# Three moved steps in a fused attention and feed-forward kernel: row loads, copies of x, a late split

## The chip, the core and the metric

The kernel runs on one core of a Trainium2 chip. A core has a matrix engine (TensorE, PE in the profile; its weight loads are PEld), a vector engine (VectorE, DVE), a scalar engine (ScalarE, ACT), GpSimd (POOL) and SyncE (SP), which here only issues DMAs. The engines run their own instruction lists and wait for one another by semaphores. The metric is the time of one execution in device microseconds.

## The reference, cut to what matters

```python
xn = _layernorm(x, axis=-1)            # x: 1 x 2048 x 512, f32
s = _A_ref(xn, A_wqkv, A_wo)           # softmax attention, 32 heads of 16
g = _silu(_B_ref(xn, ...))             # (silu(xn @ w_gate) * (xn @ w_up)) @ w_down
return x + s * g
```

## The kernel before, in words

All products are made on TensorE from values split in two parts (a high part rounded for the engine and the low remainder), three matmuls for each product. The 2048 tokens are four blocks of 512 (`NB`), each of four tiles of 128 (`NT`).

**The first stage** (L779 to L880) normalises x, transposes it and makes q, k and v, block by block. A block has twelve slots, `n` = 0 to 11, each one tile of work on TensorE with twelve 128x512 matmuls: eight feature tiles (`feature_tile`, L738, four of q and four of k) and four value tiles (`value_tile`, L753). In block 0 the value tiles come first; in the others they come last, n = 8 to 11. Around each slot the loop hands small steps to the other engines:

- `load_tile` (L541) reads 128 rows of x into `xin` (the tile `facc` in the profile), which has room for one block. `load_x` (L544) does it for four tiles. SyncE issues these loads in program order between the stores of q and k (`q_d`, `k_d`, L749).
- `stats` and `rates` (L610, L615) are mean and variance of the rows on VectorE, with a square root on ScalarE.
- Block 1 is normalised by `norm` (L628, VectorE, into `xn`, two buffers), one tile at a time, transposed on TensorE (`turn_x`, L655, by L638) and split (L649 ScalarE, L652 VectorE). Blocks 2 and 3 are normalised in place by `norms` (L663, ScalarE), transposed in sixteen pieces on VectorE (`turn_quarter`, L671, into `xw`) and split by `split_block` (L676), four casts on ScalarE (L679) and four subtractions on VectorE (L680).
- `copy_fx` (L771, ScalarE, L777) copies block 0's transposed x in sixteen pieces into `fx`, the layout of the feed-forward part. The source of the copies is the buffer that block 2 is split into.
- `feature_tile` has ScalarE square the sums and cast them (L745, L746), VectorE subtract (L747) and SyncE store both parts. The products stand in `ps`, which has four buffers; `parts` has four buffers too.
- While weights last, `split_w` (L565) has ScalarE cast a weight tile (L574) and GpSimd subtract (L575).

**The second stage** is attention, cut in 101 steps (`run`, numbered by `now`), with the feed-forward products and, from step 89 on, the output projection laid between the score matmuls (L187). The output projection of block b (`project_out`) takes steps 89 to 92 for b = 0, 93 to 96 for b = 1 and 97 to 100 for b = 2, twelve pairs of matmuls in each step. Its left operands, written (b, c), are the attention output split in two parts by `split_out` (L323), a cast and a subtraction on VectorE, queued in `chores` and run between the copies `pr<-acc` of scores (L999, L1005), or at the step's end (`tidy`, L138). The dictionary in `out_splits` (L352) says at which step each split is queued; here `early` is 87, `opened[units - 2]` is 92 and `opened[units - 1]` is 96. GpSimd gates each finished output tile (L361, L362).

Of the kernel before, what the change touches and what calls it, by code (L numbers as in the profile page):

```python
# [27 lines left out]
NT = TB // P  # L28
# [15 lines left out]
EPS = 1e-5  # L44
FINE = (30,)
TURNS = (0, 0, 0, 0, 0, 2, 4, 6, 8, 10, 13, 16, 16)
QSLOT = (0, 1, 0)
KSLOT = (0, 0, 1)

# [2 lines left out]
def tile_block(ctx: ExitStack, tc: tile.TileContext, x, wqkv, wo, w_gate, w_up, w_down, out):  # L52
# [42 lines left out]
    def load_rows(dst, src, slots):  # L95
        for h in range(2):
            for s, part in enumerate(slots):
                r = h * HALF + 2 + s * DH
                sp.dma_start(dst[r:r + DH].bitcast(F32),
                             src[part].rearrange("(j h d) t -> h d j t", j=2, h=2)[h])  # L100
# [5 lines left out]
    def load_q(u, i=None):  # L106
        g, b = divmod(u, NB)
        load_rows(qst[u % 2 if i is None else i], q_d[:, g * 64:(g + 1) * 64, b * TB:(b + 1) * TB], QSLOT)

# [37 lines left out]
    def load_wd(i):  # L147
        raw = one.tile([P, D], F32, tag="wdr", name="wdr")
        sp.dma_start(raw, w_down[(i % NF) * P:(i % NF + 1) * P])
        wdr[i] = raw  # L150
# [172 lines left out]
    def split_out(b, c):  # L323
        dst, src = lhs[b, c], parts_o[b, c]

        def rest():
            dve.tensor_sub(dst[1], src, dst[0].bitcast(F32))  # L327
            ready.add((b, c))

        chores.append((2, partial(dve.tensor_copy, dst[0], src)))  # L330
        chores.append((3, rest))
# [19 lines left out]

    def out_splits():  # L352
        for b, c in {early + 1: ((0, 0), (0, 1)), early + 2: ((0, 2),), early + 3: ((1, 0),), early + 4: ((1, 1),),
                     early + 5: ((1, 2),), opened[units - 2] + 1: ((2, 0),), opened[units - 2] + 2: ((2, 1),),
                     opened[units - 2] + 3: ((2, 2),)}.get(now, ()):
            split_out(b, c)
        if now - opened[units - 1] - 2 in range(EARLY):
            gate_rest(now - opened[units - 1] - 2)
# [37 lines left out]
    def gate_rest(t):  # L396
        chores.append((3, partial(dve.scalar_tensor_tensor, facc[:, t], facc[:, t], 0.5, gate[t], op0=ALU.mult, op1=ALU.mult)))
        chores.append((3, partial(dve.tensor_add, facc[:, t], facc[:, t], last[t])))
# [59 lines left out]
    units = NG * NB  # L458
# [7 lines left out]
    now = -1  # L466
# [17 lines left out]
    early = len(sizes) - EARLY - (NB * NT - NT)  # L484

    blocks, opened = [], []
# [40 lines left out]
    with ExitStack() as pro:  # L527
# [13 lines left out]
        def load_tile(t):  # L541
            sp.dma_start(xin[:, t % NT], x[t * P:(t + 1) * P])

        def load_x(b):  # L544
            for t in range(NT):
                load_tile(b * NT + t)
# [81 lines left out]
        def norm(t, parts=1):  # L628
            xn[t] = two.tile([P, D], F32, tag="ga", name="xn")
            n = D // parts  # L630
            for i in range(parts):
                w = slice(i * n, (i + 1) * n)
                made = dve.tensor_scalar(xn[t][:, w], xin[:, t, w], mv[:, t, 0:1], rs[:, t:t + 1], op0=ALU.subtract, op1=ALU.mult)
            return made
# [137 lines left out]
        def copy_fx(i):  # L772
            i, w = divmod(i, 2)
            i, u = divmod(i, 2)
            j, h = divmod(i, 2)
            dst = fx[halves[h], j].rearrange("p (c u) t -> u p c t", u=2)[u]
            nc.scalar.copy(dst[:, 2 * w:2 * w + 2], xt[0][j][halves[u], 2 * w:2 * w + 2])  # L777

        pend = []  # L779

        def add():
# [8 lines left out]
        for b in range(NB):  # L790
            more = b + 1 < NB
            slots = [(feature_tile, m) for m in range(8)]
            slots = [(value_tile, t) for t in range(NT)] + slots if b == 0 else slots + [(value_tile, t) for t in range(NT)]
            for n, (make, i) in enumerate(slots):
                if b == 0:
                    if n + 5 < 12:
                        load_w(worder[n + 5])
                    if n >= 2 and n + 2 < 12:
                        split_w(worder[n + 2], pool)
                if b == 0 and n == 2:  # L800
                    load_x(1)
                if more and b:
                    for part in range(TURNS[n], TURNS[n + 1]):
                        turn_quarter(part)
                if b == 2 and n in (6, 7):
                    load_gu(n - 6)
                if b == 2 and n == 8:
                    load_wd(0)
                if not more and n == 2:
                    split_gu(0)  # L810
                    tidy()
                    for bank in acc:
                        dve.memset(bank, 0.0)
                if not more and n in (1, 3):
                    load_k(0, n // 2)
                if not more and n == 5:
                    load_q(0)
                if not more and n == 6:
                    for c in range(2):
                        load_v(0, c)  # L820
                made = make(b, i)
                if b == 0 and n == 2:
                    split_x(0, 0, xf)
                if b < 2 and 0 <= 12 * b + n - 3 < 16:
                    copy_fx(12 * b + n - 3)
                if n == 0 and b:
                    flush(b - 1)
                if make is feature_tile:
                    pend.append(made)
                if b == 0 and n == 11:  # L830
                    ring(0, 2, one)
                    queries(0, one)
                if more and b:
                    if n < 2:
                        stats(2 * n)
                        stats(2 * n + 1)
                    if n == 1:
                        rates(0, NT)
                    if n in (2, 3):
                        norms(2 * n - 4)  # L840
                    if n == 10:
                        split_block(b + 1)
                elif more:
                    if 2 <= n < 6:
                        stats(n - 2)
                    if n == 5:
                        rates(0, NT)
                    if 6 <= n < 10:
                        norm(n - 6)
                    if 7 <= n < 11:  # L850
                        turn_x(b + 1, n - 7)
                if n == 10 and b < 2:
                    load_x(b + 2)
                if n == 8 and not more:
                    flush(b)
                if not more and n == 8:
                    dve.reduce_max(pk, peak, axis=AX.X)
                    dve.tensor_add(sm, pk[:, 0:1], pk[:, 1:2])
                if not more and n == 9:
                    tops = pps.tile([P, 512], F32, tag="ps", name="tops")  # L860
                    nc.tensor.transpose(tops[0:1, :P], sm, ident)
                    dve.reduce_max(s4, tops[0:1, :P], axis=AX.X)
                    dve.tensor_scalar(s4, s4, 0.51, None, op0=ALU.mult)
                    dve.tensor_scalar(flag, s4, LIMIT, None, op0=ALU.is_le)
                    dve.tensor_scalar(sel[:, :NG * NB], row[:, :NG * NB], s4, None, op0=ALU.mult)
                    for h in range(2):
                        dve.tensor_copy(selq[:, h * HALF:h * HALF + 1], s4)
                    fill(3 * DC)
                    tidy()
                    low, high = [pps.tile([P, 512], F32, tag="ps", name="low") for _ in range(2)]  # L870
                    mm(high[:2 * NG * NB, :8], sel, row[:, :8], start=True, stop=True, skip_group_check=True)
                    mm(low[:HALF + 2, :8], selq, row[:, :8], start=True, stop=True, skip_group_check=True)
                    act(shift, high[:2 * NG * NB, 0:1].to_broadcast([2 * NG * NB, 512]), AF.Copy, scale=-1.0)
                    for h in range(2):
                        two_rows = slice(h * HALF, h * HALF + 2)
                        act(qst[0][two_rows], low[two_rows, None, 0:1].to_broadcast([2, 2, 512]), AF.Copy, scale=-1.0)
                    for j in range(4):
                        pool.dma_start(sh_d[:, j * 512:(j + 1) * 512], shift.bitcast(F32))
                    fast = nc.values_load(flag, min_val=0, max_val=1)
# [53 lines left out]
    now = 0  # L933
# [93 lines left out]
    for now, (u, first, n) in enumerate(blocks):  # L1027
        g, b = divmod(u, NB)
# [101 lines left out]
```

## Time and profile before

| what | value |
|---|---|
| median of 3 runs | 1403.2 us (1402.9 to 1404.54) |
| the profiled execution, its own time | 1403.09 us |
| its span, first to last instruction | 1401.3 us |
| TensorE busy | 1392.0 us, 99% |
| ScalarE / VectorE / GpSimd busy | 1089.7 / 772.9 / 90.6 us |
| TensorE share of the chain that ended last | 87% |
| granted TensorE clock | 1.000 |

A row of the timeline reads: start in us, duration in us (of the whole group where there are several), engine, line of the kernel, operation, what is written and read, shapes, the count, and in brackets how long the engine had been idle before it and whose work ended the wait. A row of a table by windows gives the busy time of each engine in that stretch, the clock, the DMA share and GB/s. Matmuls overlap one another, so the step from one start to the next is the measure of TensorE's pace.

### The profile page before, as it was taken

Reading aid. Unit: us, or ns where it says so; the run is one execution under the profiler, and the core shown is the slowest. Engines: PE = TensorE matmul, PEld = TensorE weight load, DVE = VectorE, ACT = ScalarE, POOL = GpSimd, SP = SyncE. Lnnn points to the kernel's source line nnn. Section 1 sums busy time; section 2 is a strip of 40 time slices with the busy share of each in tenths; the row PEclk is TensorE's granted clock in tenths of the full one; section 3 lists DMA queues with packets and bytes.
Section 4 is the critical chain, followed back from the end, with each engine's and each line's share of the span. In section 5 each row is a group of like instructions: output and inputs, shape, how many; then the busy total and the mean of one; then the engine's idle time right before and its main releaser. Section 6 shows DMA issues by size and latency. Waiting matters only on the chain.

```text
span 1401.3 us, 27683 instructions
## 1 busy us (share of the span) xinstructions
PE 1392.0 (99%) x11193; PEld 841.9 (60%) x11193; DVE 772.9 (55%) x1301; ACT 1089.7 (78%) x1245; POOL 90.6 (6%) x104
## 2 busy tenths in 40 slices
PE   9999999999999999999999999999999999999998
PEld 7777756655655665565556556655565565565554
DVE  6575555355645653556456635554565446556655
ACT  6753578778888877787888778778877887788885
POOL 4200200000000000000000000000000000000333
PEclk9999999999999999999999999999999999999999
DMA  7678741043534511254514303356234113224423
GB/s 227 233 265 262 184 114 43 13 109 88 128 91 115 121 43 36 50 132 96 138 53 112 93 13 73 76 146 146 61 73 113 34 46 73 66 88 141 125 99 113
DMA packets 126954, 148.14 MB, mean 106 GB/s; under 512 B 12524, under 2 KB 79340, under 8 KB 126052
## 3 DMA queue, kind: packets, MB, share of 16 engines
q1 hardware_dynamic: 121620, 125.79, 35.0%
q0 software_dynamic: 4912, 20.12, 3.8%
q8 instruction: 89, 1.46, 0.4%
q14 instruction: 45, 0.37, 0.1%
q10 hardware_dynamic: 288, 0.39, 0.1%
HBM read 106.68 MB, written 39.58 MB: 104 GB/s over the span
## 4 chain that ended last, share of the span: by engine, by line
PE 87%; DVE 0%; ACT 0%; issue 0%; DVEq 0%
PE acc L405 32%; PE bankx L187 25%; PE score L940 17%; PE banky L187 10%; PE acc L940 3%; ACT pr L946 0%; PE acc L1067 0%; PE banky L1067 0%; PE score L1067 0%; DVE wd L143 0%; DVE wd L327 0%; DVE y L1074 0%; DVE y L368 0%; DVE pr L1005 0%; DVE pr L999 0%
## 5 line engine op out<-in xcount | busy, mean ns | idle before, releaser
L946 ACT ACTIVATE pr<-score 128x1024 f32<-128x1024 f32 x856 | 810.6, 1031 | 229.1 <-PE score L940 227.9
L405 PE MATMUL acc<-pr,vst 128*17 128x512 f32 x4096 | 461.9, 593 | 0.0
L940 PE MATMUL score<-qst,kst 50*128 50x512 f32 x1712 | 390.9, 413 | 0.1
L187 PE MATMUL bankx<-fx,guh 64*128 64x512 f32 x896 | 333.4, 393 | 0.1
L187 PE MATMUL banky<-fx,guh 64*128 64x512 f32 x896 | 324.7, 393 | 0.0
L405 PEld LDWEIGHTS acc<-pr,vst 128*17 128x17 f32 x4096 | 108.6, 97 | 286.3 <-issue 262.3
L940 PEld LDWEIGHTS score<-qst,kst 50*128 50x128 f32 x1712 | 175.2, 184 | 148.7 <-issue 68.9
L999 DVE COPY pr<-acc 128x512 f32<-128x512 f32 x168 | 116.2, 692 | 190.9 <-PE acc L940 187.1
L187 PE MATMUL bankx<-wd,hh 64*128 64x512 f32 x672 | 200.0, 392 | 0.0
L187 PE MATMUL banky<-wd,hh 64*128 64x512 f32 x672 | 197.7, 392 | 0.0
L187 PEld LDWEIGHTS bankx<-fx,guh 64*128 64x128 f32 x896 | 166.4, 186 | 19.3 <-issue 0.9
L187 PE MATMUL banky<-fx,gul 64*128 64x512 f32 x448 | 175.3, 391 | 0.0
L187 PE MATMUL bankx<-fx,gul 64*128 64x512 f32 x448 | 175.3, 391 | 0.0
L1013 ACT ACTIVATE pr<-pr 128x1024 f32<-128x1024 f32 x168 | 172.5, 1078 | 0.0
L187 PEld LDWEIGHTS banky<-fx,guh 64*128 64x128 f32 x896 | 166.3, 186 | 4.5
L1005 DVE COPY pr<-acc 128x512 f32<-128x512 f32 x168 | 116.1, 691 | 72.7 <-PE acc L940 57.2
L240 DVE SCALAR_TENSOR_TENSOR ga<-th,bankx 128x512 f32<-128x512 f32 x56 | 38.5, 688 | 178.5 <-ACT th L239 178.5
L940 PE MATMUL acc<-qst,kst 50*128 50x512 f32 x336 | 135.1, 402 | 0.3 <-DVE pr L999 0.3
L187 PEld LDWEIGHTS bankx<-wd,hh 64*128 64x128 f32 x672 | 124.9, 186 | 12.3
L187 PEld LDWEIGHTS banky<-wd,hh 64*128 64x128 f32 x672 | 124.4, 186 | 4.1
L187 PEld LDWEIGHTS bankx<-fx,gul 64*128 64x128 f32 x448 | 83.6, 187 | 11.8
L187 PEld LDWEIGHTS banky<-fx,gul 64*128 64x128 f32 x448 | 83.5, 186 | 2.3
(180 smaller groups left out, 1324.9 us busy)
## 6 DMA issues: line engine op xcount, KB each, us to landing
gur<-in_B_w_gate_dram SPq DMA_DIRECT2D x56, 256.0 KB
gur<-in_B_w_up_dram SPq DMA_DIRECT2D x56, 256.0 KB
wdr<-in_B_w_down_dram SPq DMA_DIRECT2D x56, 256.0 KB
kst<-k_d SPq DMA_DIRECT2D x192, 64.0 KB
qst<-q_d SPq DMA_DIRECT2D x192, 64.0 KB
fx<-xt_d SPq DMA_DIRECT2D x24, 512.0 KB
q_d<-parts SPq DMA_DIRECT2D x16, 512.0 KB
k_d<-parts SPq DMA_DIRECT2D x16, 512.0 KB
```

What stands on the lines that cost most here:

```text
L187: mm(banks[i], lhs[halves[i]], rhs[halves[i]], start=start, stop=stop)
L240: dve.scalar_tensor_tensor(ga, th, 1.0, bankx, op0=ALU.add, op1=ALU.mult)
L405: mm(acc[0][h * 32:h * 32 + DH + 1], v[:, kt % CT, h * (DH + 1):(h + 1) * (DH + 1)], probs[kt, h // 2][:, h % 2], start=kt == 0, stop=kt = ...
L940: mm(bank, k[r, j, kc * P:(kc + 1) * P], qst[u % 2][r, j], start=True, stop=True)
L946: act(pr, score[slot], AF.Exp, scale=0.25)
L999: dve.tensor_copy(probs[kt, j][:, 0], spare_bank)
L1005: dve.tensor_copy(probs[kt, j][:, 1], spare_bank)
L1013: act(probs[kt, j], probs[kt, j], AF.Exp, scale=0.25)
```

## The change

Four edits, all of order; no instruction is added or taken away.

1. Block 2's four row loads leave `load_x` at n = 10 of block 0 and are issued one by one at n = 7, 8, 9, 10, each behind the step that last reads its part of `xin`.
2. Block 1's `norm` of tiles 0 and 1 moves from n = 6 and 7 to n = 5 and 6; tiles 2 and 3 stay at 8 and 9.
3. The sixteen `copy_fx`, one a slot from n = 3 of block 0 to n = 6 of block 1, are spread by the table `COPIES`: six in block 0 (n = 3, 4, 5, 6, 10, 11), ten in block 1 (one each at n = 0, 1, 4, 5, 6, 7, two each at n = 8 and 9).
4. Four of the splits of the output projection move: (1, 2) from step 92 to 93, (2, 0) from 93 to 94, (2, 1) from 94 to 95, (2, 2) from 95 to 97.

```diff
+COPIES = ((0, 0, 0, 1, 1, 1, 1, 0, 0, 0, 1, 1), (1, 1, 0, 0, 1, 1, 1, 1, 2, 2, 0, 0))
...
         for b, c in {early + 1: ((0, 0), (0, 1)), early + 2: ((0, 2),), early + 3: ((1, 0),), early + 4: ((1, 1),),
-                     early + 5: ((1, 2),), opened[units - 2] + 1: ((2, 0),), opened[units - 2] + 2: ((2, 1),),
-                     opened[units - 2] + 3: ((2, 2),)}.get(now, ()):
+                     early + 6: ((1, 2),), early + 7: ((2, 0),), early + 8: ((2, 1),), early + 10: ((2, 2),)}.get(now, ()):
...
+        copied = list(range(16))
...
-                if b < 2 and 0 <= 12 * b + n - 3 < 16:
-                    copy_fx(12 * b + n - 3)
+                for _ in range(COPIES[b][n] if b < 2 else 0):
+                    copy_fx(copied.pop(0))
...
-                    if 6 <= n < 10:
-                        norm(n - 6)
+                    if n in (5, 6, 8, 9):
+                        norm((5, 6, 8, 9).index(n))
                     if 7 <= n < 11:
                         turn_x(b + 1, n - 7)
-                if n == 10 and b < 2:
+                        load_tile(2 * NT + n - 7)
+                if n == 10 and b == 1:
                     load_x(b + 2)
```

On VectorE, in block 0 from n = 5 to n = 8, stood before (`rs` is the last of `rates`, `xn` a normalised tile, `parts` the second half of a feature tile, `xt` the low part of block 1's transposed x):

```order
L626 SCALAR_TENSOR_TENSOR rs_168<-nw_169,rs_168 128x4
L747 TENSOR_TENSOR parts_400<-ps_387,parts_400 128x512
L633 TENSOR_SCALAR xn_407<-facc_83,mv_165,rs_168 128x512
L747 TENSOR_TENSOR parts_424<-ps_411,parts_424 128x512
L633 TENSOR_SCALAR xn_431<-facc_83,mv_165,rs_168 128x512
L652 TENSOR_TENSOR xt11_163<-acc0_80,xt10_162 128x4x128
```

And now, at the same place:

```order
L626 SCALAR_TENSOR_TENSOR rs_168<-nw_169,rs_168 128x4
L633 TENSOR_SCALAR xn_383<-facc_83,mv_165,rs_168 128x512
L747 TENSOR_TENSOR parts_402<-ps_389,parts_402 128x512
L633 TENSOR_SCALAR xn_409<-facc_83,mv_165,rs_168 128x512
L747 TENSOR_TENSOR parts_426<-ps_413,parts_426 128x512
L652 TENSOR_TENSOR xt11_163<-acc0_80,xt10_162 128x4x128
```

Each of the two normalisations stands one feature subtraction earlier. On SyncE, at the end of block 0, stood before the last q store, three k stores and then the four loads of rows (`facc`):

```order
L749 DMA q_d_59<-parts_424 128x2x512
L749 DMA k_d_60<-parts_454 128x2x512
L749 DMA k_d_60<-parts_484 128x2x512
L749 DMA k_d_60<-parts_512 128x2x512
L542 DMA facc_83<-in_A_x_dram 128x512 x4
```

And now:

```order
L749 DMA q_d_59<-parts_426 128x2x512
L542 DMA facc_83<-in_A_x_dram 128x512
L749 DMA k_d_60<-parts_454 128x2x512
L542 DMA facc_83<-in_A_x_dram 128x512
L749 DMA k_d_60<-parts_484 128x2x512
L542 DMA facc_83<-in_A_x_dram 128x512
L749 DMA k_d_60<-parts_512 128x2x512
```

The fourth load follows the last of these stores, where the first one stood. On VectorE, in steps 92 and 93 (`wd` holds the parts of block 1's operands and `hh` those of blocks 0 and 2; the first three rows belong to step 92 and the rows from the first L999 on to step 93), stood before:

```order
L451 TENSOR_TENSOR wd<-o,wd 128x512
L143 CAST wd<-wd 128x512
L327 TENSOR_TENSOR wd<-wd 128x512
L999 COPY pr<-acc_81 128x512
L1011 CAST hh<-hh 128x512
L1005 COPY pr<-acc_81 128x512
L327 TENSOR_TENSOR hh<-hh 128x512
```

And now (line numbers of the changed kernel are one or two higher here):

```order
L451 TENSOR_TENSOR wd<-o,wd 128x512
L1001 COPY pr<-acc_81 128x512
L1013 CAST wd<-wd 128x512
L1007 COPY pr<-acc_81 128x512
L328 TENSOR_TENSOR wd<-wd 128x512
```

The split of (1, 2) has left the end of step 92 and stands between the copies of step 93, in the place of (2, 0). In step 97, between the two copies L1001 and L1007, there is now the cast of (2, 2), and behind L1007 its subtraction, where nothing stood.

## The prediction

> **What bounds the kernel now.** I read the page first, then a table by windows for the stretches that the diff touches, then the timelines of TensorE, VectorE, ScalarE, GpSimd and SyncE there. The page says that TensorE is the bound:
>
> ```profile
> span 1401.3 us, 27683 instructions
> PE 1392.0 (99%) x11193; PEld 841.9 (60%) x11193; DVE 772.9 (55%) x1301; ACT 1089.7 (78%) x1245; POOL 90.6 (6%) x104
> ```
>
> So the change can only win what TensorE loses by waiting, and 9.3 us of idle time (1401.3 less 1392.0) is nearly all there is. The windows say where it lies (columns: TensorE, its weight loads, VectorE, ScalarE and GpSimd busy, clock, DMA share, GB/s):
>
> ```profile
> 20.00:35.00 15.00, 14.60 (x66) 11.54 (x65) 8.46 (x19) 12.56 (x20) 7.22 (x6) 1.00 0.67 215
> 45.00:60.00 15.00, 14.88 (x70) 11.12 (x69) 8.09 (x19) 7.54 (x13) 4.87 (x6) 1.00 0.95 348
> 80.00:100.00 20.00, 18.59 (x84) 14.19 (x84) 13.12 (x28) 11.29 (x21) 1.96 (x3) 1.00 0.87 317
> 1320.00:1340.00 20.00, 19.73 (x163) 9.85 (x152) 14.62 (x21) 16.98 (x19) 7.00 (x7) 1.00 0.33 100
> ```
>
> TensorE is idle for 0.40, 0.12, 1.41 and 0.27 us there, 2.2 us of the 9.3; the clock is full. Idle time hides a little more, since a matmul's row is longer than the step to the next one, so I measure stalls from start to start. Two of them in the first stage:
>
> ```profile
> 31.55 0.40 PE L694 MATMUL ps<-xt,wl 128*128 128x512 f32 x1
> 32.35 0.66 PE L638 MATMUL acc<-ident,xn 128*128 128x128 f32 x4 [0.40 <-DVE xn L633]
> ...
> 79.32 0.63 PE L696 MATMUL ps<-vh,xt 128*128 128x512 f32 x2
> 79.79 0.40 PE L696 MATMUL ps<-vl,xt 128*128 128x512 f32 x1
> 81.37 0.50 PE L694 MATMUL ps<-xt,wh 128*128 128x512 f32 x1 [1.18 <-ACT xt L679]
> 82.10 0.50 PE L694 MATMUL ps<-xt,wh 128*128 128x512 f32 x1 [0.23 <-DVE xt L680]
> 82.44 0.39 PE L694 MATMUL ps<-xt,wl 128*128 128x512 f32 x1
> ```
>
> Undisturbed, two steps take 0.47 us (79.32 to 79.79), so one takes 0.235. The first transposes of block 1 come 0.80 after the matmul before them, a loss of 0.56 us. Block 2's first three steps take 2.65 us (79.79 to 82.44) where 0.70 would do, a loss of 1.95 us.
>
> **Term 1, the start of block 2.** The chain that leads there, on SyncE, VectorE and ScalarE:
>
> ```profile
> 44.52 2.46 SPq L542 DMA_DIRECT2D facc<-in_A_x_dram  x4
> ...
> 55.38 0.69 DVE L612 BATCH_NORM_STATS2 st<-facc 128x6 f32<-128x512 f32 x1 [1.36 <-DMA facc<-in_A_x_dram]
> 57.82 0.69 DVE L612 BATCH_NORM_STATS2 st<-facc 128x6 f32<-128x512 f32 x1 [1.53 <-DMA facc<-in_A_x_dram]
> 66.26 1.41 DVE L673 STREAM_TRANSPOSE xw<-facc 32x512 f32<-32x512 f32 x2 [1.93 <-ACT facc L667]
> 74.94 5.73 DVE L673 STREAM_TRANSPOSE xw<-facc 32x512 f32<-32x512 f32 x8
> ...
> 58.77 0.30 ACT L617 ACTIVATE nw<-mv,small 128x4 f32<-128x4 f32 x1 [4.40 <-DVE mv L613]
> 71.55 1.05 ACT L777 CAST fx<-xt 64x1024 fp32r<-64x1024 f32 x1
> 77.42 0.59 ACT L764 COPY vt<-ps 128x512 f32<-128x512 f32 x1 [2.21 <-PE ps L696]
> 80.70 2.18 ACT L679 CAST xt<-xw 128x512 fp32r<-128x512 f32 x4 [2.69 <-DVE xw L673]
> ```
>
> The four loads are issued together from 44.52, into a stretch with a DMA share of 0.95. VectorE waits 1.36 us for the third tile and 1.53 us for the fourth; the square root, the normalisation and the sixteen transposes are late after it; the last transpose ends at 80.67, ScalarE casts at 80.70, and TensorE waits.
>
> Now the loads go out one feature tile apart (about 3.25 us), the last where the first stood, so near 44.5 and the first near 34.5. What a load takes there is not shown. Bounds: the first of today's four had landed when VectorE came to it, at most 7 us after issue; the last took 57.82 less about 46.5, 11.3 us. By the first the fourth tile is there by 51.6, by the second at 55.8. I take the first, since that load stands at the same place in the queue. VectorE comes to the third tile at 55.38 - 1.36 = 54.0 and needs about 0.8 us for each, so the square root starts at 55.7 instead of 58.77 (56.8 at the far end).
>
> Behind it, two squares, two casts and four normalisations of ScalarE stand in a row; the two copies that stood between (n = 2 and 3) are gone. By their rows' lengths, with a wait of some 0.8 us for VectorE's subtraction that a copy used to cover, the last normalisation ends near 61.8 instead of 66.2. The transposes are interleaved with the subtractions of features n = 4 to 7, and the last eight follow that of n = 7. TensorE ends n = 7 four slots of 2.8 us before 79.79, near 68.6; a square, a cast and a subtraction (0.6, 0.6 and 0.7 us) with their hand-overs take 2.4 us, an estimate from such rows, so the eight transposes (5.73 us) run from 71.0 to 76.7, four us sooner. Even the far landing leaves that end as it is.
>
> Then ScalarE is next. Its value copy for n = 10 waits for TensorE, at 77.42. Ahead of it stand now the value copy of n = 9 (near 74.6, a slot sooner) and two copies of 1.05 us: 74.6 + 0.6 + 2.1 = 77.3, which just fits. The casts start at 78.0, the first ends at 78.6, and VectorE's low part follows by 79.4. TensorE wants them at 80.0 and 80.25, and later pieces 0.70 us apart against 0.62 for making them. **The whole 1.95 us goes**, with 0.9 us to spare.
>
> **Term 2, block 1's first transposes.** VectorE, then GpSimd:
>
> ```profile
> 29.97 1.27 DVE L626 SCALAR_TENSOR_TENSOR rs<-nw,rs 128x4 f32<-128x4 f32 x1
> 31.76 0.53 DVE L633 TENSOR_SCALAR xn<-facc,mv,rs 128x512 f32<-128x512 f32 x1
> 37.54 0.54 DVE L633 TENSOR_SCALAR xn<-facc,mv,rs 128x512 f32<-128x512 f32 x1
> ...
> 29.92 1.29 POOL L575 TENSOR_TENSOR wl<-wraw,wh 128x512 fp32r<-128x512 f32 x1 [2.44 <-ACT wh L574]
> 39.18 1.29 POOL L575 TENSOR_TENSOR wl<-wraw,wh 128x512 fp32r<-128x512 f32 x1 [2.10 <-ACT wh L574]
> ```
>
> The normalisation ends at 32.29 and TensorE starts at 32.35. Put ahead of the feature subtraction it starts when the row at 29.97 ends, 31.24, and ends near 31.8; TensorE starts at 31.87. **That wins 0.48 us** of the 0.56 (bounds 0 and 0.56). The subtraction moved behind it frees its `ps` buffer half a us later, four slots before it is wanted: nothing. SyncE's row load for tile 0 waits for that normalisation, done 2.5 us before the load's turn: nothing either. The copies removed from n = 7 to 9 give ScalarE room where TensorE does not wait for it. The 0.12 us of 45 to 60 stays, because the copy at n = 10 stays ahead of the last cast of block 1.
>
> The row at 29.97 is a 128x4 operation that takes as long as GpSimd's subtraction beside it. The Trainium skill (SBUF — State Buffer, "Who interferes with whom") has a rule for it: a VectorE instruction with two SBUF inputs or in a two-port mode and a GpSimd instruction exclude each other, whoever starts first, for the whole instruction. The row agrees. By that rule the moved normalisations are exposed too; it gives a rival below.
>
> **Term 3, the late split.** VectorE, then GpSimd, then TensorE in steps 92 to 94:
>
> ```profile
> 1321.61 1.51 DVE L143 CAST wd<-wd 128x512 fp32r<-128x512 f32 x1
> 1325.33 0.41 DVE L1011 CAST hh<-hh 128x512 fp32r<-128x512 f32 x1
> ...
> 1321.18 1.65 POOL L361 TENSOR_TENSOR y<-y,facc 128x512 f32<-128x512 f32 x1 [5.09 <-DVE y L368]
> ...
> 1323.30 0.50 PE L187 MATMUL bankx<-fx,wd 64*128 64x512 f32 x1
> 1325.46 0.49 PE L940 MATMUL acc<-qst,kst 50*128 50x512 f32 x1 [0.27 <-DVE pr L999]
> 1328.50 1.05 PE L405 MATMUL acc<-pr,vst 128*17 128x512 f32 x8
> ...
> 1332.85 0.50 PE L187 MATMUL bankx<-fx,wd 64*128 64x512 f32 x1
> 1337.51 1.05 PE L405 MATMUL acc<-pr,vst 128*17 128x512 f32 x8
> ```
>
> The cast of (1, 2) takes 1.51 us beside GpSimd instead of 0.41, the copy of scores behind it is late, and TensorE waits for that copy at 1325.46. Step 93 takes 5.20 us to the values (1323.30 to 1328.50), step 94, with the same work, 4.66. Step 93 will have the list that step 94 has, so 0.54 us goes. Step 97 gets a cast and a subtraction:
>
> ```profile
> 1360.69 0.69 DVE L999 COPY pr<-acc 128x512 f32<-128x512 f32 x1 [2.46 <-PE acc L940]
> 1362.06 0.69 DVE L1005 COPY pr<-acc 128x512 f32<-128x512 f32 x1 [0.68 <-PE bankx L187]
> ...
> 1363.49 0.39 PE L187 MATMUL bankx<-fx,hh 64*128 64x512 f32 x1
> ```
>
> The cast (0.41) fits in the 0.68 us between the copies. The subtraction runs from 1362.7 to 1363.35, and the last pair, at 1363.49, takes it as weights, which load some 0.2 us sooner: 0 to 0.2 us late, I take 0.1. **Net 0.44 us** (bounds 0 and 0.54).
>
> **The sum** is 1.95 + 0.48 + 0.44 = 2.87 us. The stretch between the stalls is unchanged, so what lies behind each of them moves up with TensorE. From the profiled execution's 1403.09 that gives 1400.2; the median shown is 0.1 above that execution, so **1400.3 us**. About 0.2% (2.8 us, 1400.4) is what a measurement of this kernel can tell from no change; the forecast lies on that line.
>
> **The rivals.**
>
> *The moved normalisations meet GpSimd.* With the copies at n = 7 to 9 gone, ScalarE casts the weights of n = 9 some 1.2 us sooner (two copies, 2.1 us, less a wait for TensorE that then shows), so GpSimd's subtraction moves from 39.18 to near 37.6 with term 2. The normalisation of tile 2, now at 37.54, comes near 37.1, half a us ahead. If it loses, it waits 1.29 us, ends at 39.4, and TensorE, which wants it at 32.35 + 2 x 3.25 less 0.48 = 38.4, stands about 1.1 us. Total 1401.4. The skill's rule named above is the mechanism. For it: margins of half a us. Against: the normalisation is first by my count. 0.10.
>
> *ScalarE is late with block 2's casts.* The five steps before 78.0 fit with 0.1 us to spare, the casts with 0.9. If ScalarE runs 2 us late from the earlier slots, 1.1 us of term 1 is kept as a stall: 1401.4. Against: it idles 2.21 and 2.69 us there now. 0.08.
>
> *The late split only moves its stall.* If GpSimd or the tight end of step 97 costs what step 93 did, term 3 is nothing: 1400.7. 0.07.
>
> *It does not do what it says.* If block 2 starts late for another reason, such as the transposes ending where they do now, terms 2 and 3 alone are left: 1402.3. The 8.7 us from 66.26 to 74.94 on VectorE speak for it, the wait of 1.93 us at 66.26 against it. 0.05.
>
> *Slower.* A row load waits for a normalisation at the head of SyncE's queue, and the k stores wait behind it; `parts` has four buffers, so a store may be late by roughly 5 us (four slots less the flight) before ScalarE's casts stop, then `ps`, then TensorE. The normalisations end 2.5 to 3 us before the loads' turn, so it decides from about 8 us of lateness; each us beyond is a us lost. At 6 us beyond, 1406. 0.04.
>
> **How the numbers follow.** The forecast has 0.66. It straddles the line and scatter decides (the three runs span 1.6 us): 0.44 of it faster, 0.22 the same. The first four rivals, 0.30 together, are within 0.2%, the last is slower. Faster 0.44, same 0.52, slower 0.04. The range goes from 1399.3 (all bounds at their best, 3.05 us, and 0.8 of scatter) to 1402.3, which takes in the rivals up to 1401.4 with 0.9 of scatter and the fourth at its edge.
>
> **What would show it.** Right: no brackets on VectorE's four statistics near 52 to 56; the casts L679 start by 78 and TensorE goes from the last value tile into block 2 in steps of 0.235; the first transposes come 0.3 after the matmul before; step 93 takes 4.66 us. Wrong: a 1.8 us normalisation beside GpSimd near 37 to 39, a bracket on TensorE naming L679 or L680, or a wait for L328 in step 97.

## The result, and the profile after

| | before | after |
|---|---|---|
| median of 13 runs each, same chip | 1403.07 us (1402.66 to 1404.58) | 1400.01 us (1399.64 to 1400.56) |
| ratio of the two | | 0.9976, 95% interval 0.9968 to 0.9985 |
| the profiled execution, its own time | 1403.09 us | 1399.78 us |
| its span | 1401.3 us | 1398.0 us |

The changed kernel is 3.06 us faster by the medians; 2.87 was forecast. The page after and the same four windows:

```profile
span 1398.0 us, 27683 instructions
...
PE 1391.3 (100%) x11193; PEld 842.4 (60%) x11193; DVE 770.5 (55%) x1301; ACT 1088.8 (78%) x1245; POOL 90.8 (6%) x104
```

```profile
20.00:35.00 15.00, 15.00 (x68) 11.99 (x67) 9.10 (x20) 12.13 (x20) 7.75 (x7) 1.00 0.65 215
...
45.00:60.00 15.00, 14.87 (x69) 11.35 (x69) 8.46 (x22) 10.37 (x17) 4.68 (x6) 1.00 0.84 320
80.00:100.00 20.00, 20.00 (x93) 15.63 (x92) 12.97 (x29) 9.66 (x19) 1.93 (x3) 1.00 0.82 312
1320.00:1340.00 20.00, 20.00 (x164) 10.97 (x157) 10.60 (x18) 16.88 (x18) 8.42 (x9) 1.00 0.28 93
```

The span is 3.3 us shorter, with the same number of instructions. In three of the four windows TensorE now has no idle time left; in 45 to 60 it keeps what it had. The two stalls of the first stage, on TensorE:

```profile
31.47 0.39 PE L694 MATMUL ps<-xt,wl 128*128 128x512 f32 x1
31.81 0.65 PE L638 MATMUL acc<-ident,xn 128*128 128x128 f32 x4
...
79.25 0.39 PE L696 MATMUL ps<-vl,xt 128*128 128x512 f32 x1
79.47 0.63 PE L694 MATMUL ps<-xt,wh 128*128 128x512 f32 x2
79.94 0.40 PE L694 MATMUL ps<-xt,wl 128*128 128x512 f32 x1
```

The transposes start 0.34 us behind the matmul ahead of them (0.80 before), and from the last value matmul into block 2 the three steps take 0.69 us (2.65 before); no bracket is left. VectorE, which led there:

```profile
31.20 0.55 DVE L633 TENSOR_SCALAR xn<-facc,mv,rs 128x512 f32<-128x512 f32 x1
...
36.99 0.54 DVE L633 TENSOR_SCALAR xn<-facc,mv,rs 128x512 f32<-128x512 f32 x1
...
54.21 0.66 DVE L612 BATCH_NORM_STATS2 st<-facc 128x6 f32<-128x512 f32 x1
...
61.14 1.41 DVE L673 STREAM_TRANSPOSE xw<-facc 32x512 f32<-32x512 f32 x2 [0.73 <-ACT facc L667]
...
70.31 5.73 DVE L673 STREAM_TRANSPOSE xw<-facc 32x512 f32<-32x512 f32 x8
```

The fourth statistic (54.21) has no wait for a DMA, and the last transpose ends at 76.04 instead of 80.67. ScalarE behind it:

```profile
55.12 0.30 ACT L617 ACTIVATE nw<-mv,small 128x4 f32<-128x4 f32 x1 [1.30 <-DVE mv L613]
...
74.67 1.99 ACT L777 CAST fx<-xt 64x1024 fp32r<-64x1024 f32 x2
76.87 0.59 ACT L764 COPY vt<-ps 128x512 f32<-128x512 f32 x1 [0.21 <-PE ps L696]
77.48 2.18 ACT L679 CAST xt<-xw 128x512 fp32r<-128x512 f32 x4
```

The square root comes at 55.12 (58.77 before). The two copies end at 76.66, ahead of the value copy, which still waits 0.21 us for TensorE; the casts follow at 77.48 instead of 80.70. At the late split, VectorE and then TensorE:

```profile
1322.00 0.42 DVE L1013 CAST wd<-wd 128x512 fp32r<-128x512 f32 x1
1322.67 0.69 DVE L1007 COPY pr<-acc 128x512 f32<-128x512 f32 x1 [0.26 <-PE acc L942]
...
1359.38 0.68 DVE L328 TENSOR_TENSOR hh<-hh 128x512 fp32r<-128x512 f32 x1
```

```profile
1320.55 0.49 PE L188 MATMUL bankx<-fx,wd 64*128 64x512 f32 x1
...
1325.19 1.05 PE L405 MATMUL acc<-pr,vst 128*17 128x512 f32 x8
...
1329.54 0.50 PE L188 MATMUL bankx<-fx,wd 64*128 64x512 f32 x1
...
1360.11 0.18 PEld L188 LDWEIGHTS bankx<-fx,hh 64*128 64x128 f32 x1 [0.18 <-DVE hh L328]
1360.20 0.41 PE L188 MATMUL bankx<-fx,hh 64*128 64x512 f32 x1
```

The cast of (1, 2) takes 0.42 us instead of 1.51, and step 93 takes 4.64 us to its values instead of 5.20. In step 97 the weights of the last pair wait 0.18 us for the moved subtraction; the pair itself starts 3.64 us into the step, as in the kernel before. At the old place the subtraction of (1, 2) was held up too, beside GpSimd's next instruction. In the kernel before:

```profile
1322.91 1.35 POOL L362 TENSOR_TENSOR pair<-y,pair 128x512 f32<-128x512 f32 x1
1323.15 1.65 DVE L327 TENSOR_TENSOR wd<-wd 128x512 fp32r<-128x512 f32 x1
```

It takes 0.68 us in the changed kernel. With the usual 0.42 and 0.68 us the old split would have been over by about 1322.7 (an estimate from these rows). The scores of step 93 come later: the changed kernel copies them 0.84 us into the step, which would have been 1324.14. So by the rows the two delays beside GpSimd, and not the place at the end of step 92 as such, made the copy late; no run keeps the split there without GpSimd beside it.

TensorE's list holds the same 11193 matmuls in the same order in both kernels, so the time between two fixed matmuls can be compared across all kernels. Four such intervals, each from start to start, in us:

- **A**, block 1's first transposes: from the matmul ahead of them to the first feature matmul behind them (before 31.55 to 32.76).
- **B**, the start of block 1: six steps from its first matmul (before 45.31 to 47.10).
- **C**, the start of block 2: from the last value matmul to block 2's fifth (before 79.79 to 82.89; five undisturbed steps are 1.17).
- **D**, from the first `bankx` matmul of step 93 to that of step 94 (before 1323.30 to 1332.85).

| kernel | A | B | C | D | median, us | before, same chip | ratio, 95% interval |
|---|---|---|---|---|---|---|---|
| before | 1.21 | 1.79 | 3.10 | 9.55 | 1403.07 | | |
| after | 0.75 | 1.78 | 1.16 | 8.99 | 1400.01 | 1403.07 | 0.9976 [0.9968, 0.9985] |
| e1_loads_only | 1.20 | 1.77 | 1.16 | 9.56 | 1401.40 | 1402.79 | 0.9986 [0.9977, 0.9995] |
| e2_copies_only | 1.23 | 1.76 | 1.96 | 9.55 | 1401.52 | 1402.79 | 0.9987 [0.9978, 0.9996] |
| e3_old_copies | 0.75 | 1.77 | 1.16 | 9.00 | 1400.03 | 1402.79 | 0.9980 [0.9971, 0.9989] |
| e4_split_only | 1.20 | 1.77 | 2.87 | 8.99 | 1402.66 | 1403.18 | 1.0000 [0.9991, 1.0009] |
| e5_stores_later | 1.20 | 1.77 | 3.12 | 9.55 | 1403.03 | 1402.79 | 1.0001 [0.9992, 1.0010] |
| e6_copy_n9 | 0.74 | 1.39 | 1.16 | 8.99 | 1399.79 | 1403.18 | 0.9975 [0.9966, 0.9984] |
| e7_gpsimd_busy | 0.75 | 1.48 | 1.16 | 8.98 | 1400.12 | 1403.18 | 0.9982 [0.9972, 0.9991] |
| e8_norm_only | 0.73 | 1.78 | 3.18 | 9.57 | 1403.47 | 1403.18 | 1.0005 [0.9996, 1.0014] |
| e9_stores_behind | 1.21 | 1.75 | 1.16 | 9.57 | 1401.88 | 1403.59 | 0.9985 [0.9976, 0.9995] |

By these intervals the change wins 0.46 us in A, 1.94 in C and 0.56 in D, and gives 0.02 back in step 97 (from its first `bankx` matmul to that of step 98: 7.45 before, 7.47 after; the kernels without edit 4 lie between 7.45 and 7.48): **2.94 us**. The other 0.4 us of the profiled spans lies where no edit is: the first part up to A is 0.08 us shorter and most of attention, between two fixed matmuls (at 158.50 and 1273.93 us before), is 0.25 shorter (1115.42 and 1115.17). Over all eleven traces, these two scatter from 31.45 to 31.95 us and from 1115.13 to 1115.93 us, whatever the edit. So an edit worth half a us is read from its interval, and the median of its runs says little. C scatters too while the loads land late: it is 2.87 in e4 and 3.18 in e8, whose edits do not touch it.

### The profile page after: what moved, and what is told of

It is laid out like the page before. It is cut to its first block, busy times and chain, and to the rows that moved or that the text cites. A ratio compares the mean times of both kernels' runs of the same rounds, so it can differ in the third digit from the quotient of the medians.

```text
span 1398.0 us, 27683 instructions
## 1 busy us (share of the span) xinstructions
PE 1391.3 (100%) x11193; PEld 842.4 (60%) x11193; DVE 770.5 (55%) x1301; ACT 1088.8 (78%) x1245; POOL 90.8 (6%) x104
## 4 chain that ended last, share of the span: by engine, by line
PE 88%; ACT 0%; DVE 0%; issue 0%; DVEq 0%
PE acc L405 32%; PE bankx L188 23%; PE score L942 17%; PE banky L188 12%; PE acc L942 3%; ACT pr L948 0%; PE acc L1069 0%; PE banky L1069 0%; PE score L1069 0%; DVE y L1076 0%; DVE y L1082 0%; DVEq L1128 0%
## 5 line engine op out<-in xcount | busy, mean ns | idle before, releaser
L1001 DVE COPY pr<-acc 128x512 f32<-128x512 f32 x168 | 116.3, 692 | 193.2 <-PE acc L942 191.4
L1007 DVE COPY pr<-acc 128x512 f32<-128x512 f32 x168 | 116.2, 691 | 72.2 <-PE acc L942 61.3
```

The source lines that it names most:

```text
L1001: dve.tensor_copy(probs[kt, j][:, 0], spare_bank)
L1007: dve.tensor_copy(probs[kt, j][:, 1], spare_bank)
```

## The experiments

The theory: the three terms are independent stalls, and in block 2 the four loads, issued together into busy queues, set the end. The rivals were that another edit, the copies above all, wins that time, and that the normalisations collide with GpSimd.

### e1_loads_only: edit 1 alone on the kernel before

```diff
                     if 7 <= n < 11:
                         turn_x(b + 1, n - 7)
+                        load_tile(2 * NT + n - 7)
-                if n == 10 and b < 2:
+                if n == 10 and b == 1:
```

> The kernel before with edit 1 alone: block 2's row loads one by one at n = 7 to 10 of block 0, each behind the normalisation that last reads its rows; norms, copies and splits as before. Theory (the late landing of tiles 3 and 4 is the whole cause of block 2's stall, and the copies are not needed for it): VectorE's four statistics run without a wait, the square root starts near 55.7 instead of 58.77, the casts L679 wait only for the value copy and start near 78.0, the three steps into block 2 take 0.7 us instead of 2.65: 1.95 us faster than before. Rival (the copies at n = 2 and 3 of block 1 still hold the normalisations up so far that the transposes end late): the casts start near 79, and 1 us or more of the stall is kept: 1 us faster or less.

C fell to 1.16 us: the early loads alone take the whole stall. ScalarE of e1, whose copies stand where they stood before:

```profile
77.56 0.59 ACT L764 COPY vt<-ps 128x512 f32<-128x512 f32 x1 [2.21 <-PE ps L696]
78.17 2.18 ACT L679 CAST xt<-xw 128x512 fp32r<-128x512 f32 x4
```

The casts follow the value copy at once; the transposes are no longer waited for. The median is 1.4 us below the kernel before, with 1.95 expected and inside the interval (0.7 to 3.2 us).

### e2_copies_only: edit 3 alone

```diff
+COPIES = ((0, 0, 0, 1, 1, 1, 1, 0, 0, 0, 1, 1), (1, 1, 0, 0, 1, 1, 1, 1, 2, 2, 0, 0))
-                if b < 2 and 0 <= 12 * b + n - 3 < 16:
-                    copy_fx(12 * b + n - 3)
+                for _ in range(COPIES[b][n] if b < 2 else 0):
+                    copy_fx(copied.pop(0))
```

> The kernel before with edit 3 alone: the sixteen copies spread by the new table, loads, norms and splits as before. Theory: the landing stays late (square root at 58.77), but the chain behind it on ScalarE loses the two copies of n = 2 and 3, 1.4 us after a wait of 0.8 us for VectorE; VectorE is busy without a gap from the first transpose to the last, so the last ends near 79.2 instead of 80.67 and the casts start near 79.3: the stall shrinks from 1.95 to 0.4 or 0.5 us, 1.45 us faster than before. Then edits 1 and 3 win much of the same time twice. Rival (the copies count for nothing, being beside other work): within 0.2 us of before, casts at 80.7.

C fell to 1.96 us. VectorE, then TensorE of e2:

```profile
58.57 0.69 DVE L613 BATCH_NORM_STATS2 st<-facc 128x6 f32<-128x512 f32 x1 [1.92 <-DMA facc<-in_A_x_dram]
```

```profile
80.64 0.50 PE L695 MATMUL ps<-xt,wh 128*128 128x512 f32 x1
81.36 0.50 PE L695 MATMUL ps<-xt,wh 128*128 128x512 f32 x1 [0.23 <-DVE xt L681]
```

The wait for the fourth tile is still there (1.92 us in this execution), and 0.8 us of the stall with it. From the square root (59.51) to the end of the last normalisation (65.49) ScalarE now needs 5.98 us instead of 7.45, 1.47 less. So edit 3 is a second, partial way to the same time: alone it wins 1.1 us of C, beside edit 1 it has nothing left to win. That is less than the 1.45 expected: in this execution the square root came 0.74 us later than in the kernel before (58.77), while A began only 0.40 us later. (The profiled execution of e2 also ended late, but behind all work on the engines: from the issue of its last output store, at 1397.20, to the end of the span 4.7 us passed, against 3.1 before. The granted clock was 1.00 up to 1390 us. The intervals lie ahead of that.)

### e3_old_copies: the changed kernel without edit 3

```diff
-                for _ in range(COPIES[b][n] if b < 2 else 0):
-                    copy_fx(copied.pop(0))
+                if b < 2 and 0 <= 12 * b + n - 3 < 16:
+                    copy_fx(12 * b + n - 3)
```

> The changed kernel with the copies put back to one a slot, so edits 1, 2 and 4 without edit 3. Theory: the casts L679 have slack either way, so nothing is lost against the changed kernel: 1400.0 us, 3.0 faster than before, and TensorE goes into block 2 without a bracket. Rival (the spread of the copies is needed for the whole gain): a bracket naming L679 or L680 at block 2's start and 0.5 to 1.5 us lost against the changed kernel.

All four intervals and the median (1400.03) are those of the changed kernel. Edit 3 does nothing in it.

### e4_split_only and e8_norm_only: edits 4 and 2 alone

```diff
-                     early + 5: ((1, 2),), opened[units - 2] + 1: ((2, 0),), opened[units - 2] + 2: ((2, 1),),
-                     opened[units - 2] + 3: ((2, 2),)}.get(now, ()):
+                     early + 6: ((1, 2),), early + 7: ((2, 0),), early + 8: ((2, 1),), early + 10: ((2, 2),)}.get(now, ()):
```

> The kernel before with edit 4 alone: the split of (1, 2) at step 93, (2, 0) at 94, (2, 1) at 95, (2, 2) at 97. Theory: step 93 takes 4.66 us from its first output product to its values instead of 5.20, step 97 loses 0 to 0.1: 0.45 to 0.55 us faster than before, nothing else moves. Rival (the stall only goes elsewhere, to step 97 or to the gating on GpSimd): step 97 is 0.3 to 0.5 us longer than 3.96 and the time is within 0.2 us of before.

D fell from 9.55 to 8.99 us, as in the changed kernel; the medians differ by 0.5 us, inside the interval.

```diff
-                    if 6 <= n < 10:
-                        norm(n - 6)
+                    if n in (5, 6, 8, 9):
+                        norm((5, 6, 8, 9).index(n))
```

> The kernel before with edit 2 alone: the normalisation of tiles 0 and 1 of block 1 one slot earlier. Theory: block 1's first transposes start 0.34 us after the matmul before them instead of 0.80, 0.46 us faster than before, and block 2's stall stays at 1.95 us because the loads still land late. Rival (the half us is given back at block 2, whose start is set by the DMA engines and not by TensorE): the stall there grows to about 2.4 us and the time is within 0.1 us of before.

TensorE of e8:

```profile
31.92 0.40 PE L694 MATMUL ps<-xt,wl 128*128 128x512 f32 x1
32.24 0.66 PE L638 MATMUL acc<-ident,xn 128*128 128x128 f32 x4
```

The transposes follow 0.32 us behind, and A fell by 0.48. C is 0.08 us longer than before, so the half us is not given back at block 2. The time shows nothing of it: the median is 0.3 us above that of before, with an interval from -0.6 to +2.0 us, and in the profiled execution the first matmul of A came 0.37 us later than in the kernel before. What edit 2 is worth is shown by the trace alone.

### e5_stores_later and e9_stores_behind: what makes the loads late

e1 shows that early loads arrive in time, not why late ones don't. In the kernel before, the four loads go out from 44.52 to 46.98, and GpSimd issues two stores of 1 MB, block 1's `xt`, in the same two microseconds. e5 meant to put these stores off:

```diff
             split_x(b, t, turn(t), between)
-            if t == NT - 1 and b:
-                store_x(b)
...
                 made = make(b, i)
+                if b == 1 and n == 3:
+                    store_x(1)
```

> The kernel before, with all four row loads together at n = 10 as before, but GpSimd's two stores of block 1's transposed x (1 MB each) moved from the end of block 0 to n = 3 of block 1. Theory (the loads are late because they share the DMA engines with these stores): the four tiles land by 51, the statistics run without a wait, and block 2's stall goes as it does with early loads: 1.8 to 1.95 us faster than before. Rival (the loads are late by their place in SyncE's own queue, behind the stores of q and k): the third and fourth statistics still wait a us or more, and no more than 0.5 us is won.

It moved them in the program, and not in time. GpSimd, then VectorE of e5:

```profile
40.33 4.13 POOL L90 MEMSET kst<- 2x1024 f32 x4
45.26 0.57 POOL L659 DMA_DIRECT2D xt_d<-xt  x1 [0.80 <-ACT xt L649]
```

```profile
57.75 0.69 DVE L612 BATCH_NORM_STATS2 st<-facc 128x6 f32<-128x512 f32 x1 [1.55 <-DMA facc<-in_A_x_dram]
```

GpSimd has little else to do there, so it took the memsets that had stood behind the stores and issued the stores at 45.26, as before. The waits stayed, and on the question e5 is inconclusive. It is a control for the next one, though: moving the memsets changes nothing. e9 issues the stores from SyncE behind block 1's fifth store of q and k. That makes them late: they go out at 65.95 and 66.47 us (near 57 was expected), behind the statistics in either case:

```diff
             split_x(b, t, turn(t), between)
-            if t == NT - 1 and b:
-                store_x(b)
...
                 made = make(b, i)
+                if b == 1 and n == 4:
+                    for j in range(2):
+                        sp.dma_start(xt_d[1, j], xt[1][j].bitcast(F32))
```

> The kernel before, its four row loads of block 2 still issued together near 44.5 us, but the two stores of block 1's transposed x (1 MB each), which GpSimd issues at 45.3 and 46.0 there, are issued by SyncE at n = 4 of block 1, near 57 us, behind the point at which VectorE waits for the third and fourth tile. Theory (the loads are late because these 2 MB are in flight with them): without them the DMA share of 45 to 55 falls below 0.95, VectorE no longer waits 1.36 and 1.53 us for the tiles, and the interval of TensorE around block 2's start falls from 3.10 to about 1.16 us, as with early loads: the time is 1.9 us less. Rival (the loads are late because of when and where they are issued, behind one another and among the stores of k and q on SyncE): both waits stay within 0.4 us of 1.36 and 1.53, the interval stays at 3.1 us and the time is that of the kernel before. A result between says which share the two have.

The window from 50 to 55 us, first of the kernel before, then of e9:

```profile
50.00:55.00 5.00, 5.00 (x23) 4.04 (x22) 3.91 (x8) 2.82 (x4) 0.54 (x1) 1.00 1.01 413
```

```profile
50.00:55.00 5.00, 5.00 (x23) 4.08 (x22) 4.83 (x11) 3.06 (x5) 0.00 (x0) 1.00 0.63 241
```

VectorE and ScalarE of e9:

```profile
54.98 0.66 DVE L612 BATCH_NORM_STATS2 st<-facc 128x6 f32<-128x512 f32 x1
```

```profile
78.19 2.18 ACT L677 CAST xt<-xw 128x512 fp32r<-128x512 f32 x4
```

The loads were issued where they were before (44.77 to 47.13), and the share of the DMA engines from 50 to 55 fell from 1.01 to 0.63. Neither the third nor the fourth statistic waits, C is 1.16 us, and the median is 1.7 us below the kernel before. So the loads were not too late in themselves; they shared the DMA engines with 2 MB that nobody waits for so soon. Edit 1 puts them ahead of these stores: in the changed kernel the last load goes out at 43.98 and the first store at 44.81, and although the share from 50 to 55 is 1.01 there as well, nothing waits.

### e6_copy_n9: the copy at n = 10 one slot sooner, in the changed kernel

```diff
-COPIES = ((0, 0, 0, 1, 1, 1, 1, 0, 0, 0, 1, 1), (1, 1, 0, 0, 1, 1, 1, 1, 2, 2, 0, 0))
+COPIES = ((0, 0, 0, 1, 1, 1, 1, 0, 0, 1, 0, 1), (1, 1, 0, 0, 1, 1, 1, 1, 2, 2, 0, 0))
```

> The changed kernel with one entry of the table moved: the copy of n = 10 in block 0 goes to n = 9, where ScalarE is idle for 1.67 us before the next square. Theory (the copy stands between the casts of feature n = 10 and the last cast of block 1's x, and with it TensorE's second matmul of block 1 waits): the two steps at the start of block 1, 0.52 and 0.33 us, become 0.235 each, 0.39 us faster than the changed kernel, 3.4 faster than before. Rival (the wait is the length of transposes, cast and subtraction themselves): the steps stay, no gain.

TensorE at the start of block 1 in the changed kernel, then in e6:

```profile
44.76 1.02 PE L694 MATMUL ps<-xt,wh 128*128 128x512 f32 x2
45.61 0.39 PE L694 MATMUL ps<-xt,wl 128*128 128x512 f32 x1
```

```profile
44.99 0.64 PE L694 MATMUL ps<-xt,wh 128*128 128x512 f32 x2
45.46 0.39 PE L694 MATMUL ps<-xt,wl 128*128 128x512 f32 x1
```

The two matmuls take 0.47 us instead of 0.85, because ScalarE's last cast of block 1 (L649) starts at 42.93 in e6 and at 43.91 in the changed kernel; the copy that stood ahead of it now fills a gap at n = 9. B is 1.39 us, six undisturbed steps being 1.41. The median is 0.2 us below that of the changed kernel, less than these runs can tell; by the trace the version is 0.39 us faster.

### e7_gpsimd_busy: three more subtractions on GpSimd around tile 2's normalisation

```diff
                         split_w(worder[n + 2], pool)
+                        for _ in range(3 if n == 8 else 0):
+                            pool.tensor_sub(wl[:, 7], wraw[6], wh[:, 6].bitcast(F32))
```

> The changed kernel with three more GpSimd subtractions of weights at n = 8 of block 0, into a weight tile that is written properly afterwards, so GpSimd works without a pause from about 34.5 to 39.9 us, across the normalisation of tile 2 at 36.99. Theory (VectorE and GpSimd exclude each other for whole instructions, and GpSimd's next instruction goes first while it has one): the normalisation ends near 40.4, and TensorE, which wants it at 38.33, waits 2 us: 2 us slower than the changed kernel. Second theory (VectorE gets its turn between two GpSimd instructions): it starts near 37.2 and ends near 37.8, TensorE does not wait, 0 to 0.1 slower. Rival (no exclusion): the normalisation runs at 36.99 in 0.54 us.

VectorE, GpSimd and TensorE of e7:

```profile
37.10 0.54 DVE L633 TENSOR_SCALAR xn<-facc,mv,rs 128x512 f32<-128x512 f32 x1
...
40.32 1.50 DVE L633 TENSOR_SCALAR xn<-facc,mv,rs 128x512 f32<-128x512 f32 x1
```

```profile
35.87 4.29 POOL L802 TENSOR_TENSOR wl<-wraw,wh 128x512 fp32r<-128x512 f32 x3
40.24 1.29 POOL L575 TENSOR_TENSOR wl<-wraw,wh 128x512 fp32r<-128x512 f32 x1
```

```profile
41.40 0.40 PE L694 MATMUL ps<-xt,wl 128*128 128x512 f32 x1
41.87 0.66 PE L638 MATMUL acc<-ident,xn 128*128 128x128 f32 x4
```

The normalisation of tile 2 ran at full speed while GpSimd had three subtractions in a row, which took 4.29 us instead of 3 x 1.29 = 3.87: it got in between the first and the second. It came just as the first ended (37.17); the second began at 37.25 and took 1.54 us. The normalisation of tile 3 came 0.08 us behind a subtraction and took 1.50 us, 0.96 more. The Trainium skill (SBUF — State Buffer, "Who interferes with whom") has whoever starts first hold the pair of memory ports that the two engines share for the whole instruction; both normalisations agree with that. The first shows besides that a queue of GpSimd's is not held as one. An instruction that had to wait shows the same in the kernel before: the cast of (1, 2) came 0.43 us behind the start of GpSimd's L361 and ended at 1323.12, while GpSimd's next instruction, L362, ran until 1324.26. In e7 TensorE lost 0.24 us at 41.87 (0.47 from start to start instead of 0.23). The end of block 1's preparation did not move for it: B is 0.30 us shorter than in the changed kernel, since the stall that e6 removes takes up the loss, and the median is the same.

## Why the prediction was right, point by point

**Term 1, right in size and by the chain named; its reason was incomplete.** 1.95 us forecast, 1.94 measured in C (1.7 to 2.0 by the kernels before, e4, e5 and e8, whose loads are late). The steps came as worked out, less the half a us that term 2 moves everything ahead: square root at 55.12 (55.7 forecast), last normalisation done at 61.1 (61.8), last transpose at 76.04 (76.7), casts at 77.48 (78.0). The two copies ahead of the value copy fitted with 0.21 us to spare, 0.1 forecast. What a load takes stayed open: the fourth tile was there when VectorE came to it at 54.21, 10.2 us behind its issue, and as the prediction said, the end of the transposes does not hang on it. Two things were not seen. The prediction counted the removal of two copies from ScalarE's row among the things that win this time; e3 shows that it wins nothing once the loads are early. And it took the lateness for that of loads issued into a busy stretch; e9 shows that it is the collision with two stores, so that moving those would have done as well.

**Term 2, right:** 0.48 forecast, 0.46 in the changed kernel and 0.48 in e8.

**Term 3, right with a cost too high and half of the reason:** 0.54 forecast for step 93, 0.56 measured; 0.1 for step 97, 0.02 measured, which is within the scatter of that step. The wait for L328, which the prediction named as a sign of being wrong, is there (0.18 us on the weights' load), but it costs nothing: the subtraction ends at 1360.06, and the last pair starts at 1360.20, no later in its step than before. The net is 0.54 instead of 0.44. For the late copy the prediction named the cast alone, which lost 1.09 us beside GpSimd; the subtraction behind it lost another 0.97.

**The sum, right:** 2.87 forecast, 2.94 by the intervals, 3.06 by the medians. That is 0.24% of the time. The prediction put its forecast on a line of 0.2%, and the measured interval, 0.15 to 0.32%, reaches to both sides of that line.

**"The 0.12 us of 45 to 60 stays"** held, and was mis-sized. That is the idle time in a table of busy time, where a row of 0.39 us covers more than the step of 0.235 us to the next matmul and so a part of each wait; from start to start it is 0.38 us (0.85 less 0.47), as e6 shows. The prediction measured its other stalls from start to start and this one not.

**The rivals.** The moved normalisation of tile 2 ran at 36.99 to 37.53, and GpSimd's subtraction came at:

```profile
37.44 1.29 POOL L575 TENSOR_TENSOR wl<-wraw,wh 128x512 fp32r<-128x512 f32 x1 [1.61 <-ACT wh L574]
```

That is 0.45 us behind the start of the normalisation, and the margin was forecast as half a us. The price set on losing (1.1 us of TensorE) was not met when e7 made tile 3 lose: 0.24 us there, and nothing at the end of block 1. Tile 3 is a fair test, since TensorE wants either tile 0.78 us behind the usual end of its normalisation (38.31 and 41.54 in the changed kernel). The price was too high by its own rows as well: a normalisation that is ready at 37.1 loses only to a subtraction that has started by then, and so ends by 38.9, not 39.4. That ScalarE is late with the casts, that the late split moves its stall, and that the change does not do what it says are refuted by C and D; the queue of SyncE cost nothing, since the steps behind it kept their pace (from the end of A to the start of B 12.55 us before and 12.54 after, from the end of B to the start of C 32.69 and 32.71).

## What to carry to other kernels

Before a late transfer is issued sooner, look at what else was issued in the same two microseconds: here 2 MB of stores that nobody waited for made four loads late, and putting off the stores was worth as much as hurrying the loads. Count two edits on one chain together, not one by one: early loads take 1.94 us alone, spread copies 1.1 alone, both 1.94 (in the changed kernel). Measure every stall from start to start, since a matmul's row is longer than the step to the next one and covers a part of a wait, and where an edit is worth less than the scatter, compare the time between two fixed instructions instead of the whole.

## What the runs showed of the hardware

Exclusion between VectorE and GpSimd goes by the instruction: with three GpSimd subtractions queued, a VectorE normalisation ran after the first, in its usual 0.54 us, and a cast that had waited for one GpSimd instruction did not wait for the next. So far as these runs show, the price was bounded by one GpSimd instruction: 0.96 us for a normalisation beside one of 1.29 us, 1.09 us for a cast beside one of 1.65 us. And the span has two sources of scatter that no edit here touches, up to 0.5 us before the first transposes of block 1 and up to 0.8 us in 1115 us of attention, at a mean granted clock of 0.999 to 1.000 in each traced execution.
